# Scratch tiles of the router in half a PSUM bank, a second buffer for positions, and another order of the last steps but one

## The chip, the cores and the metric

The kernel runs on one core of a Trainium2 chip, as one program. The metric is the device time of an execution in microseconds. The median before is 797.3 us of 3 runs (796.97 to 798.79).

## The reference

Two stages follow each other. The first is attention in which a query sees only the keys of its own hash bucket; its output is the input `x` of a mixture of experts in which each token goes to one of eight experts.

```python
# attention: q, k, v are (4, 8, 768, 64), proj is (64, 6)
q_bucket = sum((q @ proj > 0) * 2**arange(6))          # k_bucket likewise
scores = where(q_bucket == k_bucket, q @ k.T / 8, -1e9)
attn = softmax(scores, eps=1e-9) @ v
x = attn.transpose(0, 2, 1, 3).reshape(3072, 512)
# experts: w_gate (512, 8), w1 (8, 512, 1024), w2 (8, 1024, 512)
logits = x @ w_gate + modality_bias[modality_id]
e_idx = argmax(logits); gate_w = softmax(logits, eps=1e-9)[e_idx]
out[e_idx == e] = gate_w * (relu(x @ w1[e]) @ w2[e])   # for each expert e
```

## The kernel before

**Attention.** There are 4 batches of 8 heads; two heads make a pair, so there are 16 pairs `i`, four to a batch. A loop over `i` and six key tiles `kt` runs a string of letters for each `kt` (`PLAN`, line 36; `PLAN0` for the first pair). Each letter issues one step. `S` (`score`, lines 281, 282) is a score matmul with its exponential on ScalarE (lines 293, 300); GpSimd adds the exponentials up into `sp` (line 303). `M` (`maxp`, lines 225, 231) is a matmul for the next pair, whose row maximum VectorE reduces out of a PSUM tile `psm`; there are two such tiles. `B` (`maxp_back`, lines 250 to 253) turns these maxima round on TensorE and lets VectorE write `a_0g`, `a_1g` and the flags `lone`. `T` and `P` prepare the operands of the pair after next. `A` (`weigh`, lines 322, 327) multiplies the exponentials of one key tile by `v`: first the 512 columns in the tile `psu0`, then the other 256 columns in `psu1`; ScalarE copies both to `ut` (line 332) at the end of a pair. `psu1` fills half of its PSUM bank. `Q` (`sums`, line 345) sums `sp`.

**Router.** When the four pairs of a batch are done, `finish(b)` and `route(b)` work out logits, the chosen expert and the position of every token in a table. They are generators, and a letter takes them one step on. The steps are: 1 and 2 the products with `w_gate` (line 361), 3 the sums turned round (line 371), 4 the reciprocal (373), 5 and 6 the logits of each head (386), 7 their sum `lg` (389), 8 the maximum `rm`, the difference `rd` and its exponential `rex` on ScalarE, 9 the one-hot choice `rw`, `rwm`, `oh`, 10 the matmuls 602 and 604 that count tokens, then `rk` and the counts `run`, 11 the softmax sum `rsum`, 12 the positions `pos` and, as integers, `posi`. Six more steps write six columns of records to the table `tab` in DRAM by an indirect DMA that GpSimd issues (`put`, line 624). For batches 0 and 1 these six go to a list `later`, of which the letter `s` takes one at a time; the last one of batch 1 comes in pair 13, `kt` 4. Nearly all of this is VectorE work on tiles of 6 to 48 elements a partition.

**The last batch but one.** `finish_last` (line 412) takes batch 2 through steps 1 to 12, then runs `early_slots` in six steps (13 `above`, 14 `cumulate`, 15 to 17 `assign`, 18 `early`): which experts get the two slots of 512 tokens that start before batch 3 is routed. Then `early_tables` (line 707) loads these slots' rows of `tab`, and the six `put` steps follow. Which letters take a step is in `FIN` (line 44): one row for pairs up to 11, one for pairs 12 to 15, one entry for each pair of a batch.

**What sets the order.** In attention the order on TensorE and on SyncE's DMA queue is that of the letters. On VectorE, ScalarE and GpSimd a planner sets it beforehand from its own costs and from the order in which the program names the work; a step of the router is put behind the newest reduction or flag (`newest`). Each engine then takes its instructions strictly in that order. A pool with one buffer makes the writer of a new tile wait for all readers of the old one; instructions of different engines on one PSUM tile are ordered by waits, by tile and bank and not by column. `experts` follows: slots `("e", 0)` and `("e", 1)`, into whose first the steps of batch 3 are woven, then those of the late slots.

Of the kernel before, what the change touches and what calls it, by code (L numbers as in the profile page):

```python
# [28 lines left out]
P = 128  # L29
# [6 lines left out]
PLAN = (  # L36
    "LvSPMSMSfMTfexyhk",
    "SMSMVfSMAAQTesyghk",
    "SMTSMSMlGEfxyk",
    "SMTSMSMAAFGEekk",  # L40
    "SMSMTSMgfExeshk",
    "SMTSMTSMBAABFGFfFfggehksk",
)
FIN = (("G", "g", "h", "k"), ("FG", "f", "eE", "eE"))
AHEAD = 2
PLAN0 = (
    "LvSPMSMSMT",
# [29 lines left out]
    }  # L77


def attention(ctx, actx, tc, a, x_d, route, setup, early_slots, early_tables, latest, adds, bias, later):  # L80
    nc = tc.nc
    v = a["v"]
    NPR = a.get("npair", NP)
# [231 lines left out]
    def weigh():  # L315

        for i in range(NPR):
            t = st[i]
            t["u"] = [ps_u.tile([P, MAIN], F32, name=f"psu{j}") for j in range(2)]
            for part in range(2):  # L320
                w = COLS[part].stop - COLS[part].start
                nc.tensor.matmul(t["u"][part][:, 0:w], vsb[i % 2], t["lone"][:, COLS[part]], start=True, stop=False, skip_group_check=True)
            for kt in range(NT):
                for part in range(2):
                    w = COLS[part].stop - COLS[part].start
                    for h in range(2):
# [25 lines left out]
    def finish(b):  # L352
# [26 lines left out]
        for w in range(2):  # L379
# [5 lines left out]
                nc.tensor.transpose(tp[:, j], gsb[:, tt * P:(tt + 1) * P], ident)  # L385
            nc.vector.tensor_tensor(out=gl[:, ts, 0:8], in0=tp[:, 0:n].rearrange("p t (h r) -> p t h r", r=16)[:, :, :, 0:8], in1=rin[:, ts].unsqueeze(3).broadcast_to([P, n, 8, 8]), op=ALU.mult)
            yield
        lg = bp.tile([P, NT, 8], F32, name="lg")
        nc.vector.tensor_reduce(out=lg, in_=gl.rearrange("p t h e -> p t e h"), axis=AX.X, op=ALU.add)
        yield  # L390
        yield from route(b, lg, ps_x)
# [43 lines left out]
    with tc.manual_schedule(engines={mybir.EngineType.PE, mybir.EngineType.SP}):  # L435
# [98 lines left out]
def router(ctx, tc, a, x_d, tab):  # L534
# [43 lines left out]
            nc.gpsimd.tensor_copy(out=run[0], in_=base)  # L578
            nc.gpsimd.tensor_copy(out=recs[:, :, :, 0], in_=tok)

    scattered, latest, adds, later = [], [], [], []

    def route(b, lg, ps):
        l = lg
        m = wk.tile([P, NT], F32, name="rm")
        nc.vector.tensor_reduce(out=m, in_=l, axis=AX.X, op=ALU.max)
        d = wk.tile([P, NT, E], F32, name="rd")
        nc.vector.tensor_tensor(out=d, in0=l, in1=m.unsqueeze(2).broadcast_to([P, NT, E]), op=ALU.subtract)
        ex = wk.tile([P, NT, E], F32, name="rex")
        nc.scalar.activation(ex, d, AF.Exp)  # L590
        yield
        w = wk.tile([P, NT, E], F32, name="rw")
        nc.vector.scalar_tensor_tensor(out=w, in0=d, scalar=0.0, in1=rev.unsqueeze(1).broadcast_to([P, NT, E]), op0=ALU.is_ge, op1=ALU.mult)
        wm = wk.tile([P, NT], F32, name="rwm")
        nc.vector.tensor_reduce(out=wm, in_=w, axis=AX.X, op=ALU.max)
        oh = wk.tile([P, NT, E], BF16, name="oh")
        nc.vector.tensor_tensor(out=oh, in0=w, in1=wm.unsqueeze(2).broadcast_to([P, NT, E]), op=ALU.is_equal)
        yield
        pp = ps.tile([P, HALF], F32, name="psx")
        for j in range(NT):  # L600
            lhs = tri if j == 0 else onesb
            nc.tensor.matmul(pp[:, j * E:NT * E], lhs, oh[:, 0:NT - j].rearrange("p t e -> p (t e)"), start=(j == 0), stop=False, skip_group_check=True)
        for j in range(NT):
            nc.tensor.matmul(pp[:, 64:64 + E], onesb, oh[:, j], start=False, stop=(j == NT - 1), skip_group_check=True)
        rk = wk.tile([P, NT, E], F32, name="rk")
        nc.vector.tensor_tensor(out=rk, in0=pp[:, 0:NT * E].rearrange("p (t e) -> p t e", e=E), in1=run[b % 2].unsqueeze(1).broadcast_to([P, NT, E]), op=ALU.add)
        nc.vector.tensor_tensor(out=run[(b + 1) % 2], in0=run[b % 2], in1=pp[:, 64:64 + E], op=ALU.add)
        yield
        rec = recs[:, b]
        sm = wk.tile([P, NT], F32, name="rsum")  # L610
        nc.vector.tensor_reduce(out=sm, in_=ex, axis=AX.X, op=ALU.add)
        nc.vector.tensor_scalar(out=sm, in0=sm, scalar1=1e-9, scalar2=None, op0=ALU.add)
        nc.vector.reciprocal(rec[:, :, 1].bitcast(F32), sm)
        yield
        nc.vector.tensor_tensor(out=rk, in0=rk, in1=oh, op=ALU.mult)
        pos = wk.tile([P, NT], F32, name="pos")
        nc.vector.tensor_reduce(out=pos, in_=rk, axis=AX.X, op=ALU.add)
        posi = wk.tile([P, NT], I32, name="posi")
        nc.vector.tensor_copy(out=posi, in_=pos)
        yield  # L620

        def put(t):
            with tc.issue_after(latest[0]) if b < B - 1 else nullcontext():
                ins = nc.gpsimd.indirect_dma_start(out=tab, out_offset=bass.IndirectOffsetOnAxis(ap=posi[:, t:t + 1], axis=0), in_=rec[:, t], in_offset=None).ins
            for other in scattered:
# [12 lines left out]
    early = const.tile([P, E], F32, name="early")  # L638

    def above(cnt, row, name):  # L640
        g = wk.tile([P, E, 12], F32, name="sg")
        nc.vector.tensor_tensor(out=g, in0=cnt.unsqueeze(2).broadcast_to([P, E, 12]), in1=step[:, row], op=ALU.is_gt)
        nb = wk.tile([P, E], F32, name=name)
        nc.vector.tensor_reduce(out=nb, in_=g, axis=AX.X, op=ALU.add)
        return nb

    def cumulate(nb, name):
        c2 = wk.tile([P, E, E], F32, name="sc2")
        nc.vector.tensor_tensor(out=c2, in0=low, in1=nb.unsqueeze(1).broadcast_to([P, E, E]), op=ALU.mult)
        cu = wk.tile([P, E], F32, name=name)  # L650
        nc.vector.tensor_reduce(out=cu, in_=c2, axis=AX.X, op=ALU.add)
        cx = wk.tile([P, E], F32, name=name + "x")
        nc.vector.tensor_tensor(out=cx, in0=cu, in1=nb, op=ALU.subtract)
        return cu, cx

    def assign(n, cu, cx, first, size, out):

        sel = wk.tile([P, n, E], F32, name=f"sel{n}")
        sl = slot[:, 0:n].unsqueeze(2).broadcast_to([P, n, E])
        nc.vector.tensor_tensor(out=sel, in0=cu.unsqueeze(1).broadcast_to([P, n, E]), in1=sl, op=ALU.is_gt)  # L660
        t = wk.tile([P, n, E], F32, name=f"selx{n}")
        nc.vector.tensor_tensor(out=t, in0=cx.unsqueeze(1).broadcast_to([P, n, E]), in1=sl, op=ALU.is_gt)
        nc.vector.tensor_tensor(out=sel, in0=sel, in1=t, op=ALU.subtract)
        nc.vector.tensor_tensor(out=t, in0=sel, in1=eid.unsqueeze(1).broadcast_to([P, n, E]), op=ALU.mult)
        r = wk.tile([P, n], F32, name=f"selr{n}")
        nc.vector.tensor_reduce(out=r, in_=t, axis=AX.X, op=ALU.add)
        nc.vector.tensor_copy(out=out[:, 0], in_=r)
        yield
        w = wk.tile([P, E], F32, name="selw")
        if size:  # L670
            nc.vector.tensor_tensor(out=w, in0=first, in1=cx, op=ALU.subtract)
        else:
# [11 lines left out]
    eslot = const.tile([P, 2, EARLY], I32, name="eslot")  # L684

    def early_slots():
        nb = above(run[EARLYB % 2], 0, "enb")
        yield
        cu, cx = cumulate(nb, "ecu")
        zero = wk.tile([P, E], F32, name="ezero")  # L690
        nc.vector.memset(zero, 0.0)
        yield
        yield from assign(EARLY, cu, cx, zero, TS, eslot)
        nc.vector.tensor_scalar(out=early, in0=cx, scalar1=-1.0, scalar2=float(EARLY), op0=ALU.mult, op1=ALU.add)
        nc.vector.tensor_scalar(out=early, in0=early, scalar1=0.0, scalar2=None, op0=ALU.max)
# [36 lines left out]
        nc.vector.tensor_copy(out=tot[:, 2:3], in_=over[:, 0:1])  # L732
        return big, sml, tot

    return route, early_slots, early_tables, (eslot, etb, ete), late_slots, setup, latest, adds, bias, later


def experts(ctx, tc, a, x_d, tab, out, ps_x, ident, first, adds):
# [247 lines left out]
def body(tc, a, out):  # L986
# [1 line left out]
    x_d = tc.dram_tile([N + 1, DM], F32, name="x_d")  # L988
    tab = tc.dram_tile([DUMMY + TS, 2], I32, name="tab")
    with ExitStack() as ctx, ExitStack() as actx:  # L990
        route, early_slots, early_tables, early_tiles, late_slots, setup, latest, adds, bias, later = router(ctx, tc, a, x_d, tab)
        finish, finish_x, ps_x, ident = attention(ctx, actx, tc, a, x_d, route, setup, early_slots, early_tables, latest, adds, bias, later)
        actx.close()
        runner, tabs, conditional = experts(ctx, tc, a, x_d, tab, out, ps_x, ident, early_tiles, adds)
        r = runner()
# [38 lines left out]
```

## Time and profile before

| | |
|---|---|
| median of 3 runs | 797.3 us |
| the profiled execution's own time | 798.82 us |
| its span, first to last instruction | 796.9 us |
| mean granted TensorE clock | 0.983 |
| TensorE matmuls busy | 751.4 us (94%) |
| VectorE busy | 486.7 us (61%) |
| ScalarE busy | 415.0 us (52%) |
| GpSimd busy | 444.6 us (56%) |

PE is TensorE's matmuls, PEld its weight loads, DVE VectorE, ACT ScalarE, POOL GpSimd, SP SyncE. A row of the timeline gives start, length, engine, line, operation, the tile written and read, the count, and in brackets how long the engine sat idle before it and what ended that. In a table by stretches, each engine has its busy time, and PEclk is the granted TensorE clock as a share of full speed. Attention takes the span up to about 481 us, the experts the rest.

### The profile page before, as it was taken

To read this page: it belongs to the slowest core of one execution; us is meant where nothing else is said; L and a number is where in the kernel's file an instruction comes from. 1 tells how busy PE (TensorE), PEld (TensorE's weight loads), DVE (VectorE), ACT (ScalarE), POOL (GpSimd) and SP (SyncE) were. 2 spreads that over 40 slices of the span, in tenths; PEclk is the share of its full clock that TensorE was granted. 3 is DMA by queue.
4 is the path that set the end of the run, shared out by engine and by line. 5 is a ranking of instruction groups with operands and counts; after the bars stand their busy time and mean duration, and the time that the engine had idled before them with its cause. 6 is when DMAs were issued, how large, how long until landed. Compare 5 with 4: busy or idle time off the path is not lost.

```text
span 796.9 us, 11622 instructions
## 1 busy us (share of the span) xinstructions
PE 751.4 (94%) x4060; PEld 523.7 (66%) x4060; DVE 486.7 (61%) x828; ACT 415.0 (52%) x732; POOL 444.6 (56%) x325
## 2 busy tenths in 40 slices
PE   5799999999999999999898899999999999999996
PEld 2555556556566566555555556878888888888885
DVE  5677677577777769766857758754244342752422
ACT  3666676666557566665554455324253334643323
POOL 7298988788879988789775793024220204202002
PEclk9699999999999999999999999999999999999999
DMA  5676544254347434454400366466443435853411
GB/s 193 157 181 160 159 122 133 65 159 113 111 120 177 115 81 125 117 168 108 120 21 14 83 143 233 150 82 223 132 160 90 161 103 170 267 143 121 132 55 60
DMA packets 59573, 104.11 MB, mean 131 GB/s; under 512 B 9709, under 2 KB 30957, under 8 KB 59504
## 3 DMA queue, kind: packets, MB, share of 16 engines
q1 hardware_dynamic: 53424, 88.10, 39.8%
q0 software_dynamic: 4928, 13.14, 5.2%
q10 hardware_dynamic: 1152, 2.03, 0.8%
q8 instruction: 34, 0.56, 0.3%
q14 instruction: 35, 0.29, 0.1%
HBM read 59.76 MB, written 13.33 MB: 92 GB/s over the span
## 4 chain that ended last, share of the span: by engine, by line
PE 64%; DVE 11%; issue 10%; ACT 6%; DMA 4%; POOL 2%; SPq 1%; another core or an unknown queue 1%; ACTq 0%; POOLq 0%; DVEq 0%
PE psu L327 12%; PE pss L281 8%; PE pss L282 6%; PE hps L824 5%; PE hps L825 5%; PE hps L826 5%; PE yps L868 4%; PE yps L870 4%; PE yps L869 4%; PE psm L225 3%; ACT pb L293 2%; PE psm L231 2%; DVE b_1g L162 2%; DVE a_0g L252 2%; DVE mx L227 1%
## 5 line engine op out<-in xcount | busy, mean ns | idle before, releaser
L303 POOL TENSOR_TENSOR sp<-sp,pb 128x768 f32<-128x768 f32 x124 | 232.4, 1900 | 33.0 <-ACT pb L300 30.5
L293 ACT ACTIVATE pb<-pss 128x512 f32<-128x512 f32 x192 | 114.2, 598 | 112.3 <-PE pss L282 96.2
L227 DVE TENSOR_REDUCE mx<-psm 128x1 f32<-128x512 f32 x192 | 130.6, 688 | 58.8 <-PE psm L225 57.7
L777 DVE TENSOR_TENSOR w<-raw,w 128x1024 fp32r<-128x1024 f32 x64 | 79.5, 1248 | 95.3 <-ACT w L775 63.0
L327 PE MATMUL psu<-pb,vt 128*64 128x512 f32 (+1 forms) x768 | 137.0, 499 | 0.0
L775 ACT CAST w<-raw 128x1024 fp32r<-128x1024 f32 x64 | 66.9, 1050 | 73.3 <-PE yps L870 62.7
L327 PEld LDWEIGHTS psu<-pb,vt 128*64 128x64 f32 x768 | 51.6, 139 | 71.1 <-issue 61.3
L795 POOL DMA_INDIRECT xg<-x_d,tb x18 | 21.9, 1219 | 117.8 <-DMA tb<-tab 113.6
L281 PE MATMUL pss<-a_0g 128*128 128x512 f32 x192 | 80.8, 421 | 2.6 <-ACT pb L293 1.6
L868 PE MATMUL yps<-w,hl 128*128 128x512 f32 x208 | 82.7, 398 | 0.0
L870 PE MATMUL yps<-w,hh 128*128 128x512 f32 x208 | 81.3, 391 | 0.0
L869 PE MATMUL yps<-w,hh 128*128 128x512 f32 x208 | 81.0, 389 | 0.0
L824 PE MATMUL hps<-xh,w 128*128 128x512 f32 x192 | 75.5, 393 | 0.0
L825 PE MATMUL hps<-xl,w 128*128 128x512 f32 x192 | 74.8, 390 | 0.7 <-DVE xl L814 0.7
L826 PE MATMUL hps<-xh,w 128*128 128x512 f32 x192 | 74.8, 390 | 0.0
L303 POOL TENSOR_TENSOR sp<-pb,pb 128x768 f32<-128x768 f32 x31 | 56.7, 1850 | 29.7 <-ACT pb L300 29.6
L233 DVE TENSOR_REDUCE mx<-psm 128x2 f32<-128x512 f32 x96 | 66.1, 689 | 10.2 <-PE psm L231 7.5
L281 PE MATMUL pss<-a_1g 128*128 128x512 f32 x192 | 68.3, 356 | 3.9 <-ACT pb L300 3.9
L830 ACT ACTIVATE hh<-hps 128x512 fp32r<-128x512 f32 x48 | 28.7, 598 | 74.0 <-PE hps L826 71.9
L282 PE MATMUL pss<-b_0g 128*128 128x512 f32 x192 | 66.0, 344 | 0.8 <-DMA b_0g<-a_0g 0.8
L282 PE MATMUL pss<-b_1g 128*128 128x512 f32 x192 | 65.7, 342 | 0.0
L831 DVE SCALAR_TENSOR_TENSOR hl<-hps,hh 128x512 fp32r<-128x512 f32 x48 | 33.0, 688 | 51.4 <-ACT hh L830 49.1
(203 smaller groups left out, 1363.0 us busy)
## 6 DMA issues: line engine op xcount, KB each, us to landing
raw<-moe_w SPq DMA_DIRECT2D x64, 512.0 KB
xt<-qk SPq DMA_DIRECT2D x31, 384.0 KB
vt<-v SPq DMA_DIRECT2D x16, 384.0 KB
a_0g<-hx SPq DMA_DIRECT2D x30, 192.0 KB
a_1g<-hx SPq DMA_DIRECT2D x30, 192.0 KB
x_d<-xs SPq DMA_DIRECT2D x18, 256.0 KB
b_1g<-a_1g SPq DMA_DIRECT2D x17, 192.0 KB
b_0g<-a_0g SPq DMA_DIRECT2D x17, 192.0 KB
```

Of the source, the lines that this page charges most:

```text
L227: newest[:] = [nc.vector.tensor_reduce(out=mx[:, qt + j, 1 - h, 0:1], in_=mp, axis=AX.X, op=ALU.max).ins]
L281: nc.tensor.matmul(out, t["s1"][h][:, ks], t["m1"][h][:, cs], start=True, stop=False)
L282: nc.tensor.matmul(out, t["s2"][h][:, ks], t["m2"][h][:, cs], start=False, stop=True)
L293: nc.scalar.activation(t["pb"][kt][:, h, 0:MAIN], sp, AF.Exp, scale=0.125)
L303: add = (nc.vector if h and i in CFG["spd"] else nc.gpsimd).tensor_tensor(out=t["sp"][:, h], in0=(t["pb"][0] if kt == 1 else t["sp"])[:, h ...
L327: nc.tensor.matmul(t["u"][part][64 * h:64 * h + 64, 0:w], t["v"][:, h, kt], t["pb"][kt][:, h, COLS[part]], start=False, stop=(kt == NT - 1 ...
L824: nc.tensor.matmul(hps, lo[:, c, fs], xh[:, c], start=(c == 0), stop=False)
L825: nc.tensor.matmul(hps, hi[:, c, fs], xl[:, c], start=False, stop=False)
L826: nc.tensor.matmul(hps, hi[:, c, fs], xh[:, c], start=False, stop=(c == 3))
L868: nc.tensor.matmul(yps[g], hl[fc][:, gs], hi[:, fb], start=(fc == 0), stop=False)
L869: nc.tensor.matmul(yps[g], hh[fc][:, gs], lo[:, fb], start=False, stop=False)
L870: nc.tensor.matmul(yps[g], hh[fc][:, gs], hi[:, fb], start=False, stop=(fc == 7))
```

## The change

Four things are done.

The tile `psu1` becomes one lasting tile `shared` of a whole bank; `weigh` uses its columns 0 to 255 and the router's tiles lie in columns 256 to 511 while attention runs (`Spots`; with no PSUM given it falls back to the pool). After attention the router's work uses pool tiles as before. The instructions that produced and read these tiles are the same, but for three: batch 1 writes its counts a second time into the scratch (`counts`), `cumulate` reduces a second time into a pool tile, and `early` takes two instructions in place of three. Operands are placed so that no instruction has two tensor inputs in PSUM, and nearly none has two in SBUF.

`posi` gets a second buffer.

`PLAN` gets a letter `w` behind the `G` in `kt` 2, 3 (two) and 4. `FIN` changes its row for pairs 12 to 15: in pair 12 `w` takes a step in place of `F` and `G` (4 steps in place of 7), in pair 13 `f` and `e` in place of `f` alone (12 in place of 7). So pair 12 makes steps 1 to 4 (before 1 to 7), pair 13 steps 5 to 16 (before 8 to 14), and pair 14 begins with 17 (before 15).

```diff
-    "SMTSMSMlGEfxyk",
-    "SMTSMSMAAFGEekk",
-    "SMSMTSMgfExeshk",
+    "SMTSMSMlGwEfxyk",
+    "SMTSMSMAAFwGwEekk",
+    "SMSMTSMgwfExeshk",
...
-FIN = (("G", "g", "h", "k"), ("FG", "f", "eE", "eE"))
+FIN = (("G", "g", "h", "k"), ("w", "fe", "eE", "eE"))
...
+class Spots:
+    psum = None
+    def __call__(self, pool, shape, name, at):
+        if self.psum is None:
+            return pool.tile(shape, F32, name=name)
+        n = int(np.prod(shape[1:]))
+        ap = self.psum[:, at:at + n]
+        return ap if len(shape) == 2 else ap.rearrange("p (a e) -> p a e", a=shape[1])
...
+    shared = ps_u.tile([P, MAIN], F32, name="psu1")
+    spot.psum = shared[:, REST:MAIN]
...
-            t["u"] = [ps_u.tile([P, MAIN], F32, name=f"psu{j}") for j in range(2)]
+            t["u"] = [ps_u.tile([P, MAIN], F32, name="psu0"), shared[:, 0:REST]]
...
-        lg = bp.tile([P, NT, 8], F32, name="lg")
+        lg = spot(bp, [P, NT, 8], "lg", 0)
...
         sums(NPR - 1)
+        spot.psum = None
...
-        d = wk.tile([P, NT, E], F32, name="rd")
+        d = spot(wk, [P, NT, E], "rd", 48)
...
-        w = wk.tile([P, NT, E], F32, name="rw")
+        w = spot(wk, [P, NT, E], "rw", 96)
...
-        rk = wk.tile([P, NT, E], F32, name="rk")
+        rk = spot(wk, [P, NT, E], "rk", 144)
...
+        if b == EARLYB - 1:
+            counts.append(spot(wk, [P, E], "counts", 200))
+            nc.vector.tensor_tensor(out=counts[0], in0=run[b % 2], in1=pp[:, 64:64 + E], op=ALU.add)
...
-        sm = wk.tile([P, NT], F32, name="rsum")
+        sm = spot(wk, [P, NT], "rsum", 192)
...
-        pos = wk.tile([P, NT], F32, name="pos")
+        pos = spot(wk, [P, NT], "pos", 192)
...
-        posi = wk.tile([P, NT], I32, name="posi")
+        posi = wk.tile([P, NT], I32, name="posi", bufs=2)
...
-        cx = wk.tile([P, E], F32, name=name + "x")
-        nc.vector.tensor_tensor(out=cx, in0=cu, in1=nb, op=ALU.subtract)
+        cx = spot(wk, [P, E], name + "x", 224)
+        cs = cu
+        if spot.psum is not None:
+            cs = wk.tile([P, E], F32, name=name + "s")
+            nc.vector.tensor_reduce(out=cs, in_=c2, axis=AX.X, op=ALU.add)
+        nc.vector.tensor_tensor(out=cx, in0=cs, in1=nb, op=ALU.subtract)
...
-        nc.vector.tensor_scalar(out=early, in0=cx, scalar1=-1.0, scalar2=float(EARLY), op0=ALU.mult, op1=ALU.add)
-        nc.vector.tensor_scalar(out=early, in0=early, scalar1=0.0, scalar2=None, op0=ALU.max)
-        nc.vector.tensor_tensor(out=early, in0=early, in1=nb, op=ALU.min)
+        left = wk.tile([P, E], F32, name="eleft")
+        nc.vector.tensor_scalar(out=left, in0=cx, scalar1=-1.0, scalar2=float(EARLY), op0=ALU.mult, op1=ALU.add)
+        nc.vector.scalar_tensor_tensor(out=early, in0=left, scalar=0.0, in1=nb, op0=ALU.max, op1=ALU.min)
```

The tiles `sg`, `enb`, `sc2`, `ecu`, `ecux`, `sel`, `selr` and `selw` of `early_slots` go to the scratch in the same way.

## Rows read from the trace of the kernel before

**Rows 1.** The page's first part: busy time of each engine.

```profile
PE 751.4 (94%) x4060; PEld 523.7 (66%) x4060; DVE 486.7 (61%) x828; ACT 415.0 (52%) x732; POOL 444.6 (56%) x325
```

**Rows 2.** Busy time in stretches from one `Q` to the next: pairs 4, 12, 13, 14.

```profile
142.93:171.75 28.82, 27.63 (x171) 16.43 (x169) 20.17 (x36) 17.80 (x35) 22.66 (x15) 1.00 0.41 114
...
368.31:402.74 34.43, 30.61 (x190) 18.09 (x188) 23.26 (x46) 16.71 (x35) 28.84 (x21) 0.95 0.30 77
402.74:433.78 31.04, 27.15 (x157) 17.38 (x155) 20.84 (x51) 16.58 (x33) 20.34 (x16) 0.95 0.08 23
433.78:462.52 28.74, 26.09 (x145) 15.86 (x143) 21.67 (x38) 12.89 (x25) 21.16 (x14) 0.94 0.40 110
```

**Rows 3.** Timeline of PE, 385 to 442 us: its longest waits.

```profile
388.95 0.63 PE L385 MATMUL psx<-ident,gsb 128*128 128x128 f32 x4 [0.54 <-DVE lone L253]
390.17 0.41 PE L385 MATMUL psx<-ident,gsb 128*128 128x128 f32 x2 [0.59 <-DVE lone L253]
...
397.22 0.18 PE L602 MATMUL psx<-oh,tri 128*128 128x48 bf16 x1 [2.10 <-DVE oh L597]
...
424.84 0.34 PE L208 MATMUL psx<-bits,pat 128*128 128x384 bf16 x1 [3.50 <-DVE lone L253]
...
441.92 0.53 PE L231 MATMUL psm<-a_1g 128*128 128x256 f32 x2 [2.38 <-DVE mx L227]
```

**Rows 4.** Stretches right behind three waits: stretch, length, engines, PEclk, DMA, GB/s.

```profile
397.20:402.80 5.60, 5.58 (x38) 2.81 (x41) 1.19 (x4) 0.97 (x2) 3.57 (x2) 0.70 0.01 1
...
424.85:428.60 3.75, 3.75 (x16) 3.39 (x16) 3.33 (x10) 2.15 (x4) 0.00 (x0) 0.55 0.00 0
...
441.90:447.00 5.10, 5.08 (x20) 2.11 (x20) 3.34 (x9) 0.63 (x1) 2.87 (x2) 0.67 0.01 1
```

**Rows 5.** Timeline of DVE, 394 to 397 us.

```profile
394.04 1.20 DVE L588 TENSOR_TENSOR rd<-lg,rm 128x48 f32<-128x48 f32 x1
...
396.96 0.21 DVE L597 TENSOR_TENSOR oh<-rw,rwm 128x48 bf16<-128x48 f32 x1
```

**Rows 6.** Timeline of DVE, 424 us.

```profile
424.02 0.17 DVE L619 CAST posi<-pos 128x6 int32<-128x6 f32 x1 [4.18 <-DMA tab<-recs,posi]
424.10 0.68 DVE L253 TENSOR_SCALAR lone<-psx 128x512 fp32r<-128x512 f32 x1
```

**Rows 7.** Timeline of POOL, 419 to 480 us.

```profile
419.49 0.98 POOL L624 DMA_INDIRECT tab<-recs,posi  x1
...
437.62 7.15 POOL L303 TENSOR_TENSOR sp<-sp,pb 128x768 f32<-128x768 f32 x4 [2.32 <-ACT pb L300]
449.04 0.98 POOL L624 DMA_INDIRECT tab<-recs,posi  x1 [4.27 <-DMA x_d<-xs]
...
473.09 6.89 POOL L303 TENSOR_TENSOR sp<-sp,pb 128x768 f32<-128x768 f32 x3
```

**Rows 8.** Timeline of DVE, 433 to 445 us: four long small instructions.

```profile
433.64 1.69 DVE L674 SCALAR_TENSOR_TENSOR selw<-selw,ke 128x8 f32<-128x8 f32 x1
...
437.80 1.71 DVE L677 SCALAR_TENSOR_TENSOR selx<-kslot,selw 128x16 f32<-128x16 f32 x1
...
440.03 1.23 DVE L678 TENSOR_TENSOR selx<-selx,sel 128x16 f32<-128x16 f32 x1
...
443.55 1.25 DVE L681 CAST eslot<-selr 128x2 int32<-128x2 f32 x1
```

**Rows 9.** Three lines' instructions over all batches: shortest, median and longest ns.

```profile
L588 DVE TENSOR_TENSOR rd<-lg,rm x4: 198/203/1199, 196.2 to 503.7; 128x48 f32<-128x48 f32 x4
...
L606 DVE TENSOR_TENSOR rk<-psx,run x4: 196/202/208, 213.0 to 514.5; 128x48 f32<-128x48 f32 x4
...
L607 DVE TENSOR_TENSOR run<-run,psx x4: 150/152/153, 213.1 to 514.6; 128x8 f32<-128x8 f32 x4
```

**Rows 10.** Timeline of PE and ACT in pair 6, behind step 8 of batch 0.

```profile
196.90 2.80 PE L327 MATMUL psu<-pb,vt 128*64 128x512 f32 x16
...
197.61 0.24 ACT L590 ACTIVATE rex<-rd 128x48 f32<-128x48 f32 x1
```

**Rows 11.** Timeline of PE at the end of attention.

```profile
480.73 0.85 PE L345 MATMUL psx<-sp,ones 128*32 128x384 f32 x8
```

More of the change, by code (lines that the diff above doesn't have):

```diff
@@ L77, in host_layout, with attention @@
     }
-def attention(ctx, actx, tc, a, x_d, route, setup, early_slots, early_tables, latest, adds, bias, later):
+class Spots:
[6 more added lines that the diff above has]
+        return ap if len(shape) == 2 else ap.rearrange("p (a e) -> p a e", a=shape[1])
+def attention(ctx, actx, tc, a, x_d, route, setup, early_slots, early_tables, latest, adds, bias, later, spot):
     nc = tc.nc
@@ L579, in setup @@
             nc.gpsimd.tensor_copy(out=recs[:, :, :, 0], in_=tok)
-    scattered, latest, adds, later = [], [], [], []
+    scattered, latest, adds, later, counts, spot = [], [], [], [], [], Spots()
     def route(b, lg, ps):
@@ L640, in above @@
     def above(cnt, row, name):
-        g = wk.tile([P, E, 12], F32, name="sg")
+        g = spot(wk, [P, E, 12], "sg", 0)
         nc.vector.tensor_tensor(out=g, in0=cnt.unsqueeze(2).broadcast_to([P, E, 12]), in1=step[:, row], op=ALU.is_gt)
-        nb = wk.tile([P, E], F32, name=name)
+        nb = spot(wk, [P, E], name, 208)
         nc.vector.tensor_reduce(out=nb, in_=g, axis=AX.X, op=ALU.add)
@@ L647, in cumulate @@
     def cumulate(nb, name):
-        c2 = wk.tile([P, E, E], F32, name="sc2")
+        c2 = spot(wk, [P, E, E], "sc2", 96)
         nc.vector.tensor_tensor(out=c2, in0=low, in1=nb.unsqueeze(1).broadcast_to([P, E, E]), op=ALU.mult)
-        cu = wk.tile([P, E], F32, name=name)
+        cu = spot(wk, [P, E], name, 216)
         nc.vector.tensor_reduce(out=cu, in_=c2, axis=AX.X, op=ALU.add)
-        cx = wk.tile([P, E], F32, name=name + "x")
-        nc.vector.tensor_tensor(out=cx, in0=cu, in1=nb, op=ALU.subtract)
+        cx = spot(wk, [P, E], name + "x", 224)
[4 more added lines that the diff above has]
+        nc.vector.tensor_tensor(out=cx, in0=cs, in1=nb, op=ALU.subtract)
         return cu, cx
     def assign(n, cu, cx, first, size, out):
-        sel = wk.tile([P, n, E], F32, name=f"sel{n}")
+        sel = spot(wk, [P, n, E], f"sel{n}", 160)
         sl = slot[:, 0:n].unsqueeze(2).broadcast_to([P, n, E])
@@ L664, in assign @@
         nc.vector.tensor_tensor(out=t, in0=sel, in1=eid.unsqueeze(1).broadcast_to([P, n, E]), op=ALU.mult)
-        r = wk.tile([P, n], F32, name=f"selr{n}")
+        r = spot(wk, [P, n], f"selr{n}", 192)
         nc.vector.tensor_reduce(out=r, in_=t, axis=AX.X, op=ALU.add)
@@ L668, in assign @@
         yield
-        w = wk.tile([P, E], F32, name="selw")
+        w = spot(wk, [P, E], "selw", 232)
         if size:
@@ L686, in early_slots @@
     def early_slots():
-        nb = above(run[EARLYB % 2], 0, "enb")
+        nb = above(counts[0], 0, "enb")
         yield
@@ L733, in late_slots @@
         return big, sml, tot
-    return route, early_slots, early_tables, (eslot, etb, ete), late_slots, setup, latest, adds, bias, later
+    return route, early_slots, early_tables, (eslot, etb, ete), late_slots, setup, latest, adds, bias, later, spot
 def experts(ctx, tc, a, x_d, tab, out, ps_x, ident, first, adds):
@@ L990, in body @@
     with ExitStack() as ctx, ExitStack() as actx:
-        route, early_slots, early_tables, early_tiles, late_slots, setup, latest, adds, bias, later = router(ctx, tc, a, x_d, tab)
-        finish, finish_x, ps_x, ident = attention(ctx, actx, tc, a, x_d, route, setup, early_slots, early_tables, latest, adds, bias, later)
+        route, early_slots, early_tables, early_tiles, late_slots, setup, latest, adds, bias, later, spot = router(ctx, tc, a, x_d, tab)
+        finish, finish_x, ps_x, ident = attention(ctx, actx, tc, a, x_d, route, setup, early_slots, early_tables, latest, adds, bias, later, spot)
         actx.close()
```

## The prediction

> **What bounds the kernel now.** I read the engines' busy time first: TensorE's matmuls fill 94% of the span [rows 1], so the time is TensorE's work plus the holes in it. A gain must close a hole or raise the clock; busy time saved on VectorE alone gives nothing. Next I cut attention into stretches from one `Q` to the next, one a pair [rows 2]. Pair 4, a usual one with router steps, takes 28.82 us at full clock. Pair 12 takes 34.43, and pairs 12, 13 and 14 alone have a mean clock of 0.94 to 0.95. In these three runs the work that the change rearranges: batch 2's router and the early slots. The timeline of TensorE shows why they are slow [rows 3]: three long waits, 2.10, 3.50 and 2.38 us, each ended by VectorE, and two of 0.54 and 0.59. Behind each long one the granted clock sits between its two levels of 1.2 and 2.4 GHz: a mean of 0.70 over 5.60 us, 0.55 over 3.75 and 0.67 over 5.10 [rows 4]. Length times one minus clock gives 1.68, 1.69 and 1.68 us lost behind a wait. So the holes cost:
> - A, in pair 13 before the counting matmul (line 602): 2.10 + 1.68 = 3.78
> - B, at the start of pair 14 (line 208): 3.50 + 1.69 = 5.19
> - C, in pair 14 (line 231): 2.38 + 1.68 = 4.06
> - D, at the end of pair 12 (line 385): 0.54 + 0.59 = 1.13
>
> 14.16 us in all. The question is which of them the change closes, and what it opens.
>
> **The second buffer of `posi` (B).** The integer positions of batch 2 wait 4.18 us, and what ends the wait is the DMA that still reads those of batch 1 [rows 6]. Its issue on GpSimd stands at 419.49, 0.98 us long [rows 7]: the last `put` of batch 1, which the letters place in the same `kt` 4 of pair 13 as step 12. VectorE goes in order, so `lone` stands behind `posi` and starts at 424.10 [rows 6]; TensorE waits for `lone` to free its PSUM tile and starts at 424.84 [rows 3]. With two buffers batch 2 writes where nobody reads, and batch 3 takes the first buffer long after. `lone` then starts 4.2 us earlier, more than the wait is long. Nothing else is late there: the instruction before `posi` had ended by 419.84 (424.02 less 4.18). All of B goes: 5.19.
>
> **The scratch in PSUM (C, part of A).** Four small instructions of `early_slots` take 1.69, 1.71, 1.23 and 1.25 us on 2 to 16 elements [rows 8]. Lines of that size that read PSUM take 0.15 us, whatever GpSimd does; `rk` with one input in PSUM takes 196 to 208 ns in all batches, while `rd` with both inputs in SBUF takes 198 to 1199 [rows 9]. And the long ones lie beside additions on GpSimd: four from 437.62 to 444.77 [rows 7], and `selx` ends at 439.51 and at 441.26, `eslot` at 444.80, near the ends of the first, second and fourth (7.15 / 4 = 1.79 each). So these instructions wait out a GpSimd addition that reads SBUF. In hole C the two on `selx` are over by 1.71 + 1.23 - 2 x 0.17 = 2.6 us, as much as TensorE's 2.38; the reduction that it waits for stands behind them. With an operand in PSUM I expect 0.2 us each, and all of C goes: 4.06. In hole A `rd` is over by 1.0 [rows 5].
>
> What no row shows is VectorE writing PSUM. Nearest are the reads of rows 9: 0 to 10 ns dearer than the undisturbed SBUF form. I bound it by nothing and, as a long form, by the whole 0.2 us of such an instruction again; some 60 instructions are moved, of which about 20 lie in the crowded start of pair 14, so 0 to 4 us there. I take 0, by the nearest row.
>
> The Trainium skill has a rule against this (Perfetto Trace Analysis, Optimizing Scalar/DVE Operations): about 60 ns of overhead per VectorE instruction on SBUF and 125 on PSUM. The median `rk` of 202 against 203 ns of `rd` [rows 9] shows no such step for a read. By the rule 20 instructions would cost an estimated 1.3 us more, 787.7 in place of my 786.4.
>
> **The other rhythm (rest of A, D).** Before, steps 8, 9 and 10 follow each other in `kt` 0 and 1 of pair 13. The counting matmul stands ready at 395.12 (397.22 less 2.10), `oh` starts at 396.96 [rows 3, 5]; 1.0 us off `rd` would leave a hole of about 1.1. After, step 9 is at the end of `kt` 1 and the matmul at the end of `kt` 2, a whole key tile apart (about 28.8 / 6 = 4.8 us), so the rest closes too: A gives 3.78. Steps 4 to 7 leave `kt` 5 of pair 12, where line 385 met the tiles that `lone` still held; their place in `kt` 3 to 5 and in `kt` 0 of pair 13 lies 3 us behind `lone`. But the pattern matmul of the next pair then meets the same tiles. Between 0 and 1.13 I take half: 0.6.
>
> Together 5.19 + 4.06 + 3.78 + 0.6 = 13.6 us.
>
> **What it adds.** (1) Two instructions more, one less, on VectorE: one in all, of 0.15 us by the shortest line of [rows 9], in the start of pair 14: 0.15. (2) New waits. Scratch and `psu1` are now one tile in one bank, so the second part of each `A` waits for every scratch instruction named before it, and those named after it wait for the `A` and the copy to `ut`. A waiting `A` holds all of TensorE. I count 13 places where a scratch step lies between two groups of `A`: 4 in each of batches 0 and 1, 5 in the last. The nearest is step 8: before, `rex` in pair 6 ends at 197.85 [rows 10]; the first `A` there starts at 196.90, half of 2.80 us, its `psu1` part being the last third, thus at 197.83. So it is level. Elsewhere the letters leave most of a `kt`. I take 0.1 each, 1.3 us, between 0 and, where all were like the waits of D, 13 x 0.57 = 7.4. VectorE's own waits for `A` come where it has nothing else (behind `Q`). (3) Steps 14 to 17 crowd into the end of pair 13 and `kt` 0 of pair 14, beside `lone` and the reductions. Before, VectorE kept up there while TensorE ran at 0.55 clock [rows 4]; at full clock TensorE is 1.69 us sooner, so the cost is 0 to 1.7. I take 1.0. (4) `early_tables` moves from `kt` 3 of pair 14 to `kt` 2, `put` with it. On SP its two DMAs and the `x_d` writes queued behind come sooner; on GpSimd the first `put` waited 4.27 us at 449.04 [rows 7], which the row gives to `x_d`, but the DMA that reads `tab` had to land first, issued just before. (5) GpSimd's last three additions end at 479.98 [rows 7], 0.75 before the last `Q` [rows 11]. If TensorE comes 12 us sooner, they must as well. Between, GpSimd idles 2.32 + 4.27 [rows 7] and pair 14 has 21.16 busy of 28.74 [rows 2], so it can; I take 0.3, at most 3.
>
> Sum: 13.6 - 0.15 - 1.3 - 1.0 - 0.3 = 10.9 us off. What follows is TensorE-bound and moves along, its weight loads too, as they are freed by attention's end. The profiled execution took 798.8 (span 796.9 and 1.9 around it): 787.9 after. It lies 1.5 above the median of 797.3, so the forecast median is 786.4.
>
> **The rivals.**
> *Partly given back.* The holes close, but the 13 meeting places cost like D's waits (7.4) in place of 1.3: 10.9 - 6.1 = 4.8, 792.5. For it: steps of 20 small instructions before one `A`. Against: rows 10.
> *The scratch doesn't help.* The long small instructions wait for GpSimd wherever their operands lie. Then A (by the rhythm) and B close, C moves with its steps and stays: 10.9 - 4.1 = 6.8, 790.5. Against it stands the narrow spread of `rk`.
> *Slower: the shared bank takes TensorE into VectorE's queue.* Place: the second part of `A`, 13 times. Price: a wait like the shortest long one, 2.10 us, without loss of clock 27.3, against 13.6 gained: 13.7 slower, 811. It decides from a mean wait of 13.6 / 13 = 1.05 us. For it: VectorE is over 70% busy in these pairs (20.17 of 28.82 [rows 2]) and in order. Against: two `psm` tiles keep VectorE within two reductions of TensorE, and only step 8 stands right before an `A`.
> The Trainium skill (PSUM — Partial Sum Buffer, PSUM bank collisions raise a hardware error) says that engines on one bank are to be kept apart by bank and not by address; by that the waits exist though the columns differ. No run here shows their length yet.
>
> **How the numbers follow.** Forecast 0.66, by itself 783 to 790; partly given back 0.14; no help from the scratch 0.06; no change 0.04; slower 0.10. The low end is all 14.16 us off the median, 783.1, and a little: 782.8. The high end takes in the second rival and most of the first: 794.5. What is left out is mostly the slower case. A measurement can tell about 0.2% (1.6 us): faster 0.86, same 0.04, slower 0.10.
>
> **What would show it.** Right: pairs 12, 13 and 14 at about 30, 27 and 25 us with clock 1.00; no DVE row waiting for `tab`; `selw`, `selx`, `eslot` at 0.2 us; the last `Q` near 470. Wrong: waits of line 327 or 322 for `rd`, `rex`, `rk` or `pos` over 1 us; `put` or the last additions of GpSimd after 472 us with TensorE waiting at line 345; small instructions still over 1 us.

## The result, and the profile after

The changed kernel takes 789.88 us in the median of 6 runs (787.76 to 790.72) against 798.04 before: ratio 0.9891, 95% interval 0.9871 to 0.9910, 8.2 us off where 10.9 were forecast. A second series on another chip gave 790.54 against 797.36, ratio 0.9917 (0.9891 to 0.9942). The profiled execution took 790.72, span 788.9.

First, where in the span the 8.0 us between the two profiles (796.9 to 788.9) lie. The sums matmul `Q` runs once a pair; these are its first starts before and after, and the last one after (the last before is in [rows 11]).

```profile
63.22 0.85 PE L345 MATMUL psx<-sp,ones 128*32 128x384 f32 x8
```

```profile
61.35 0.85 PE L359 MATMUL psx<-sp,ones 128*32 128x384 f32 x8
...
472.89 0.85 PE L359 MATMUL psx<-sp,ones 128*32 128x384 f32 x8
```

From first to last `Q` it is 417.5 us before and 411.5 after: 6.0 us. Another 1.9 lie ahead of the first `Q`, where both programs issue the same instructions in the same order on every engine; there the profile before was at clock 0.54 from 20 to 30 us, the one after at 1.00. In the 14 profiles of this study the first `Q` starts between 61.2 and 64.9 us, whatever was changed. So 1.9 us of the difference is one execution against another, and below I compare the stretch from the first to the last `Q`. The pairs after (stretch, length, engines, granted clock), to be held against [rows 2]:

```profile
365.89:395.80 29.91, 28.01 (x177) 16.86 (x176) 21.35 (x41) 16.68 (x35) 27.12 (x19) 1.00 0.36 90
395.80:427.65 31.85, 28.11 (x168) 16.81 (x166) 21.85 (x63) 16.48 (x33) 23.69 (x18) 0.95 0.07 17
427.65:452.90 25.25, 24.20 (x145) 15.26 (x143) 17.28 (x30) 13.38 (x26) 19.62 (x15) 1.00 0.57 118
```

Pairs 12 and 14 lost 4.5 and 3.5 us and run at full clock, as forecast. Pair 13 did not get faster (31.04 to 31.85). TensorE's timeline after shows why; it answers to [rows 3]:

```profile
388.03 0.60 PE L399 MATMUL psx<-ident,gsb 128*128 128x128 f32 x4
...
393.93 1.94 PE L341 MATMUL psu<-pb,vt 128*64 128x256 f32 x12 [1.52 <-ACT rex L605]
...
399.53 0.20 PE L617 MATMUL psx<-oh,tri 128*128 128x48 bf16 x1
...
413.02 1.94 PE L341 MATMUL psu<-pb,vt 128*64 128x256 f32 x12 [0.74 <-DVE psu L662]
...
424.23 3.50 PE L341 MATMUL psu<-pb,vt 128*64 128x256 f32 x12 [2.61 <-DVE eslot L703]
...
452.90 0.84 PE L359 MATMUL psx<-sp,ones 128*32 128x384 f32 x4 [0.67 <-POOL sp L317]
454.65 0.84 PE L359 MATMUL psx<-sp,ones 128*32 128x384 f32 x4 [0.92 <-POOL sp L317]
```

None of the old waits is left: the transposes (line 399) and the counting matmul (line 617) start without one, and no matmul of pairs 12 to 14 waits 0.3 us or more for `lone` or a reduction. In their place the accumulating matmuls `A` wait three times, always with their second part, which lies in the bank that the scratch shares: for step 8 (`rex` reads `rd`), 13 (line 662) and 17 (line 703). Behind the longest the clock falls:

```profile
424.30:428.00 3.70, 3.70 (x17) 1.33 (x20) 0.00 (x0) 0.81 (x2) 0.45 (x1) 0.58 0.23 71
```

That is 3.70 x 0.42 = 1.55 us more. So 1.52 + 0.74 + 2.61 + 1.55 = 6.42 us are new, and 0.67 + 0.92 = 1.59 for GpSimd's additions, 8.01 in all. 14.16 closed less 8.01 opened is 6.15, near the 6.0 measured. VectorE's timeline, against [rows 6, 8]:

```profile
410.74 0.15 DVE L637 CAST posi<-psu 128x6 int32<-128x6 f32 x1
...
422.77 0.17 DVE L696 SCALAR_TENSOR_TENSOR psu<-psu,ke 128x8 f32<-128x8 f32 x1
...
423.19 0.17 DVE L699 SCALAR_TENSOR_TENSOR selx<-kslot,psu 128x16 f32<-128x16 f32 x1
...
424.01 0.16 DVE L703 CAST eslot<-psu 128x2 int32<-128x2 f32 x1
```

No wait for the table's DMA, and 0.17 us where there were 1.7.

### The profile page after: what moved, and what is told of

The parts are those of the page before. It is cut to its first block, busy times and chain, and to the rows that moved or that the text cites. A ratio compares the mean times of both kernels' runs of the same rounds, so it can differ in the third digit from the quotient of the medians.

```text
span 788.9 us, 11622 instructions
## 1 busy us (share of the span) xinstructions
PE 747.6 (95%) x4060; PEld 520.3 (66%) x4060; DVE 477.8 (61%) x829; ACT 414.8 (53%) x732; POOL 445.6 (56%) x325
## 4 chain that ended last, share of the span: by engine, by line
PE 65%; DVE 11%; issue 10%; ACT 5%; DMA 4%; POOL 3%; SPq 1%; POOLq 0%; ACTq 0%; DVEq 0%
PE psu L341 12%; PE pss L295 8%; PE pss L296 6%; PE hps L846 4%; PE hps L848 4%; PE hps L847 4%; PE yps L892 4%; PE yps L890 4%; PE yps L891 4%; PE psm L239 4%; PE psm L245 2%; ACT pb L307 2%; DVE b_1g L176 2%; PE psx L359 1%; DVE a_0g L266 1%
```

## The experiments

The kernel before took 797.2 to 797.4 us in the medians of the three series. "Wait" is what TensorE waits for VectorE's work in pairs 12 to 14 (waits from 0.3 us), "first to last" the stretch from the first to the last `Q`, both of the one profile.

| kernel | `posi` | scratch | letters | median | ratio (95%) | wait | first to last |
|---|---|---|---|---|---|---|---|
| before | 1 | no | old | 797.3 | 1 | 9.11 | 417.5 |
| changed, again | 2 | all | new | 790.54 | 0.9917 (0.9891 to 0.9942) | 4.86 | 411.7 |
| posi_alone | 2 | no | old | 796.27 | 0.9981 (0.9959 to 1.0002) | 8.04 | 414.7 |
| scratch_old_rhythm | 2 | all | old | 787.60 | 0.9865 (0.9835 to 0.9895) | 5.07 | 410.4 |
| rhythm_no_scratch | 2 | no | new | 788.32 | 0.9883 (0.9851 to 0.9915) | 2.64 | 407.7 |
| early_steps | 2 | all | earlier | 795.94 | 0.9982 (0.9965 to 0.9998) | 3.45 | 415.9 |
| step17_behind | 2 | all | one moved | 789.90 | 0.9901 (0.9881 to 0.9922) | 3.84 | 409.1 |
| spread_steps | 2 | all | spread | 784.78 | 0.9843 (0.9822 to 0.9865) | 1.50 | 403.5 |
| one_scratch | 2 | one output | new | 787.97 | 0.9880 (0.9860 to 0.9900) | 2.67 | 407.6 |
| input_scratch | 2 | one input | new | 785.30 | 0.9844 (0.9822 to 0.9866) | 0.77 | 405.9 |
| single_posi | 1 | all | new | 797.78 | 0.9999 (0.9980 to 1.0017) | 10.42 | 418.9 |
| spread_no_scratch | 2 | no | spread | 790.67 | 0.9898 (0.9872 to 0.9924) | 4.40 | 407.6 |
| spread_more | 2 | all | spread, one moved | 785.32 | 0.9847 (0.9824 to 0.9869) | 1.49 | 403.5 |

**The second buffer alone** (posi_alone).

```diff
-        posi = wk.tile([P, NT], I32, name="posi")
+        posi = wk.tile([P, NT], I32, name="posi", bufs=2)
```

> The kernel before with nothing but the second buffer of the integer positions. Theory (each hole closes by its own edit): hole B, 3.50 us of waiting and 1.69 us behind it at a lower clock, goes; holes A, C and D stay. So 5.2 us off the kernel before, 792.8 us against a median of 798.0, and no row of VectorE waits for the table's DMA. Rival (B only covers C: with lone sooner, VectorE meets GpSimd's additions at the same small instructions, and TensorE waits there as long): under 2 us off, 796 us or more, with the wait at the reductions' matmul (lines 225 to 231) grown from 2.38 us to over 4.

1.1 us off, at the edge of what can be told: the rival, with two waits of 2.46 and 2.34 us in place of one of over 4. TensorE's longest waits in this kernel, the granted clock behind each, and VectorE and GpSimd ahead of the second:

```profile
395.66 0.18 PE L602 MATMUL psx<-oh,tri 128*128 128x48 bf16 x1 [2.09 <-DVE oh L597]
...
423.72 0.51 PE L231 MATMUL psm<-a_0g 128*128 128x256 f32 x2 [2.46 <-DVE mx L227]
437.99 0.50 PE L231 MATMUL psm<-a_1g 128*128 128x256 f32 x2 [2.34 <-DVE mx L227]
```

```profile
395.70:401.00 5.30, 5.30 (x34) 2.85 (x33) 1.13 (x4) 0.85 (x2) 3.04 (x2) 0.68 0.00 2
...
424.00:429.00 5.00, 5.00 (x32) 3.46 (x33) 4.94 (x13) 2.11 (x5) 2.37 (x3) 1.00 0.15 56
...
438.00:443.00 5.00, 5.00 (x26) 2.64 (x27) 3.82 (x10) 1.23 (x2) 2.85 (x2) 1.00 0.01 1
```

```profile
420.39 2.66 DVE L642 TENSOR_TENSOR sg<-run,kstep 128x96 f32<-128x96 f32 x1
```

```profile
419.30 3.62 POOL L303 TENSOR_TENSOR sp<-sp,pb 128x768 f32<-128x768 f32 x2
```

`posi` and `lone` no longer wait, but step 13's first instruction behind them does: 2.66 us, until GpSimd's two additions end at 422.92. The wait that the DMA had caused was in series with one that GpSimd causes; taking one away shows the other.

**Scratch without the new letters, letters without the scratch.** The first takes PLAN and FIN from before, the second is the kernel before with `bufs=2` and the new PLAN and FIN.

> The changed kernel with the letters (PLAN and FIN) of the kernel before: scratch and second buffer without the rhythm. Theory 1 (the waits of the accumulating matmuls for the scratch, 1.52, 0.74 and 2.61 us in the changed kernel, come from where the new letters put steps 8, 13 and 17): other steps stand before an A here, so these three waits are gone or elsewhere; B and C close, a hole of about 1.1 us with 1.7 of clock stays before the counting matmul, and D's 1.13 us: about 788 to 792 us. Theory 2 (they come from sharing the bank, wherever the steps stand): waits of line 341 for VectorE of 4 us or more in all appear again beside the holes left of A and D, 793 us or more.

> The kernel before with the second buffer and the new letters, all small operands in SBUF. Theory 1 (the new waits are the price of the shared bank, the scratch's gain is hole C): no wait of the accumulating matmuls (line 327 here) for VectorE; the small instructions of steps 13 to 17 take over 1 us each again where GpSimd adds, and TensorE waits some 2 to 3 us (and loses 1.7 us of clock) for VectorE behind them. A and B gone, C back: 789 to 792 us, level with the changed kernel, since what the scratch gave (4.1 us) is what its bank took (6.4 us with its loss of clock). Theory 2 (the new waits come from the crowding of steps by the new letters, whatever memory the scratch is in): TensorE waits for VectorE at the same three places, 793 us or more.

Both are level with the changed kernel or a little faster. With the old letters the counting matmul waits 1.87 us, the transposes 0.55 and 0.59 (A and D), and `A` 1.39 and 0.67 for steps 15 and 17. Ahead of the counting matmul, VectorE now waits for ScalarE's `rex`, which reads `rd` in the same bank:

```profile
394.93 0.22 DVE L608 SCALAR_TENSOR_TENSOR psu<-psu,ke 128x48 f32<-128x48 f32 x1 [0.58 <-ACT rex L605]
```

```profile
396.40 0.18 PE L617 MATMUL psx<-oh,tri 128*128 128x48 bf16 x1 [1.87 <-DVE oh L612]
```

Without scratch no `A` waits for VectorE at all, and neither does the counting matmul; step 14's product takes 2.26 us, TensorE waits 1.98 behind it and 0.66 later, at full clock:

```profile
414.89 2.26 DVE L649 TENSOR_TENSOR sc<-klow,enb 128x64 f32<-128x64 f32 x1
```

```profile
417.81 0.51 PE L231 MATMUL psm<-a_0g 128*128 128x256 f32 x2 [1.98 <-DVE mx L227]
...
427.69 0.51 PE L231 MATMUL psm<-a_0g 128*128 128x256 f32 x2 [0.66 <-DVE mx L227]
```

By their waits theory 1 holds in both, though both times are a little under its ranges: with the new letters the scratch took what it gave, or more. Buffer and letters alone make up the whole gain of the changed kernel.

**Steps earlier** (early_steps): a letter `z` in place of pair 13's `f` and `e`, and two more `w` for pair 12.

```diff
-    "LvSPMSMSfMTfexyhk",
-    "SMSMVfSMAAQTesyghk",
-    "SMTSMSMlGwEfxyk",
-    "SMTSMSMAAFwGwEekk",
-    "SMSMTSMgwfExeshk",
-    "SMTSMTSMBAABFGFfFfggehksk",
+    "LvSPMSMSfzMTfzexyhk",
+    "SMSMVfSMAAQTzesyghk",
+    "SMTSMSMlGwzEfxyk",
+    "SMTSMSMAAFwzGwzEekk",
+    "SMzSMzTSMgwzfExewshk",
+    "SMTSMwTSMBAABzFGzFfFfggehksk",
...
-FIN = (("G", "g", "h", "k"), ("w", "fe", "eE", "eE"))
+FIN = (("G", "g", "h", "k"), ("w", "z", "eE", "eE"))
```

> The changed kernel with the steps of batch 2 earlier and clear of the accumulating matmuls: six steps in pair 12 instead of four; step 8 a quarter of a pair before an A, step 9 behind it, steps 13 to 15 in key tile 4 of pair 13, 16 and 17 right behind the A of key tile 5. Theory 1 (the changed kernel loses 1.52 + 0.74 + 2.61 us of waiting and 1.56 us of clock because steps 8, 13 and 17 are issued late and stand in VectorE's queue when an A wants the bank): all three waits fall under 0.3 us, and the time falls by about 6 us from the changed kernel's 789.9 to 783 to 785 us. Theory 2 (VectorE is full there and the waits only move to another place): the sum of TensorE's waits for VectorE in pairs 12 to 14 stays at 4 us or more, and the time within 2 us of 789.9.

Both theories miss: some 6 us slower than the changed kernel. None of its three waits recurs, but step 15 now stands ahead of the `A` of key tile 5, and VectorE takes its instructions between the two halves of `lone`:

```profile
418.96 2.78 PE L341 MATMUL psu<-pb,vt 128*64 128x256 f32 x12 [3.45 <-DVE eslot L689]
...
458.67 1.49 PE L359 MATMUL psx<-sp,ones 128*32 128x384 f32 x4 [3.34 <-POOL sp L317]
```

The clock behind the first is 0.66 over 5 us. GpSimd then idles 7.74 us for exponentials that come late, and its additions are 3.34 us late at pair 14's sums. Not how early a step is named counts, but whether VectorE has it done when the next `A` comes.

**Steps behind the `A`.** step17_behind moves one step, spread_steps all of batch 2 (a letter `z` for pair 13, `q` for pair 14).

```diff
-    "LvSPMSMSfMTfexyhk",
-    "SMSMVfSMAAQTesyghk",
-    "SMTSMSMlGwEfxyk",
-    "SMTSMSMAAFwGwEekk",
-    "SMSMTSMgwfExeshk",
-    "SMTSMTSMBAABFGFfFfggehksk",
+    "LvSPMSMSfzMTfzezxyhk",
+    "SMSMVfSMAAQzTezqqsyghk",
+    "SMqTSMSMlGwzEfxyk",
+    "SMTSMSMAAFwzqGwzqEekk",
+    "SMzqSMTSMgwfExeqshk",
+    "SMTSMTSMBAABzqFGqFfqFggehksk",
...
-FIN = (("G", "g", "h", "k"), ("w", "fe", "eE", "eE"))
+FIN = (("G", "g", "h", "k"), ("w", "z", "q", "eE"))
```

> The changed kernel with one step moved: step 17 stands behind the two A of key tile 1 of pair 14 instead of at the end of key tile 0. Theory (the changed kernel's wait of 2.61 us at that A is the price of sharing the bank with a step that VectorE reaches late, and the 1.56 us behind it come with it): the wait goes and 2.6 to 4.2 us with it, 785.7 to 787.3 against 789.9; VectorE waits for the copy of the sums instead, where nobody waits for VectorE. Rival (VectorE is full there, TensorE waits for it wherever the step stands): the reductions' matmul (line 245) waits instead, and the time stays within 1.5 us of the changed kernel's.

> The changed kernel with every scratch step of batch 2 placed behind an A: step 8 and 9 behind those of key tile 1 of pair 13, 11 and 12 of key tile 3, 13 early in key tile 4, 14 behind those of key tile 5, 15 and 16 behind those of key tile 1 of pair 14, 17 early in key tile 2, 18 and the tables' loads behind those of key tile 3. Theory (price of the shared bank is paid where a step stands within VectorE's delay ahead of an A): waits of line 341 for VectorE sum to under 1 us, 783 to 786 us. Rival (as the steps that were moved earlier showed: the order that the planner gives VectorE puts small steps ahead of what an A needs in any rhythm): waits of 3 us or more, 788 us or more.

> The changed kernel once more, beside the three others on one chip. All theories: within 0.2% of 789.9 us in the median; its profile shows again waits of the accumulating matmuls for VectorE at the same places (1.5, 0.7 and 2.6 us), since these follow from the order of the instructions; the loss of clock behind the last of them may or may not appear, as the run with the second buffer alone showed full clock behind two waits of 2.3 to 2.5 us.

The changed kernel repeats its waits (1.51, 0.74, 2.61, clock 0.83 from 420 to 430 us) and its stretch (411.7). With step 17 alone behind the `A`, that wait falls only to 1.59, now for step 16, with the clock kept (neither theory: it stays at the `A` but does not go); the stretch is 2.5 us shorter, the median 0.6, which these runs can't tell from nothing. With all steps behind the `A` no row of line 341 waits for VectorE; one wait of the shared bank is left, and the time is 784.8, 12.6 us under the kernel before and better than both kernels:

```profile
429.06 0.39 PE L336 MATMUL psu<-lone,vs 128*128 128x256 f32 x1 [1.50 <-DVE eslot L703]
```

> The run with the spread steps with one step moved again: step 17 from early key tile 2 of pair 14 to behind the A of key tile 1, right behind step 16. There, the second part of the A's start in key tile 3 waited 1.50 us for step 17's last instruction. Theory (the price is VectorE's delay: it reaches step 17 1.5 us late): the wait falls under 0.4 us and the time by about 1.3 us, 783.5. Rival (VectorE works at the pace of the reductions there, small steps between them end when the reductions end): the wait stays over 1 us and the time within 0.5 us of 784.8.

The rival: 785.32, and 1.49 us of wait. VectorE's rows there alternate, one reduction of 0.67 and one small instruction, so step 17 ends when they end.

**Does the scratch give anything then?** The spread letters with everything in SBUF.

> The letters of the run with the spread steps, which took 784.8 us, with all small operands in SBUF again. Theory 1 (there the letters had put the price of the bank away and left the scratch's gain): small instructions take 1 to 2 us again beside GpSimd's additions, TensorE waits 2 to 4 us for VectorE behind them, 787 to 790 us. Theory 2 (the letters alone made that run fast, the scratch gives nothing where steps are spread): within 1.5 us of 784.8, with waits for VectorE of under 2 us in all.

Theory 1, a little above its range: 790.67, 5.9 us slower than with scratch; waits of 0.86, 1.49, 0.35, 0.92 and 0.78 us, with small instructions of up to 1.81 us ahead of them.

**Which operand has to be in PSUM?** Both kernels are rhythm_no_scratch with one tile moved: one_scratch the output of step 14's product, input_scratch its second input.

```diff
-        c2 = wk.tile([P, E, E], F32, name="sc2")
+        c2 = spot[0][:, 0:E * E].rearrange("p (a e) -> p a e", a=E) if spot else wk.tile([P, E, E], F32, name="sc2")
```

```diff
+        nbp = spot[0][:, 0:E]
+        nc.vector.tensor_reduce(out=nbp, in_=nb.unsqueeze(2), axis=AX.X, op=ALU.add)
+        cu, cx = cumulate(nb, "ecu", nbp)
...
-        nc.vector.tensor_tensor(out=c2, in0=low, in1=nb.unsqueeze(1).broadcast_to([P, E, E]), op=ALU.mult)
+        nc.vector.tensor_tensor(out=c2, in0=low, in1=nbp.unsqueeze(1).broadcast_to([P, E, E]), op=ALU.mult)
```

> The new letters and the second buffer, and of all scratch only one tile in PSUM: the 8 x 8 product of step 14 (sc2). Without scratch its instruction took 2.26 us beside a GpSimd addition, and TensorE waited 1.98 us behind it. Theory (what waits out GpSimd's addition is a small instruction with all operands in SBUF; one operand in PSUM frees it, and far from an A it costs nothing): this instruction takes 0.2 us, the wait of 1.98 us goes, the sum of the waits of TensorE for VectorE in pairs 13 and 14 falls from 2.64 us to about 0.7, and the time from 788.3 to about 786. Rival (the next small instruction with operands in SBUF takes the wait over, as in the run with the second buffer alone): one of the instructions behind it takes over 1 us, TensorE waits 1.5 us or more there, 787.5 us or more.

> As the run with one tile of scratch, but the other side of the instruction: the 8 x 8 product of step 14 is written to SBUF, and its second input, the 8 numbers before it, is read from a copy in PSUM that one more reduction writes. With the product written to PSUM and both inputs in SBUF that instruction took 2.29 us and TensorE waited 2.02 us. Theory 1 (what waits out GpSimd's addition is an instruction that reads all its tensors from SBUF; where it writes doesn't matter): now 0.2 us, and the wait of 2.0 us is gone or under 0.5; the stretch from the first sums to the last, 407.6 us in the profile of that run, falls to 405 to 406. Theory 2 (it waits as soon as one operand of two is in SBUF, and what helped in the changed kernel was that the small instructions stand elsewhere in time): it takes over 1 us again and the wait of about 2 us stays.

GpSimd and VectorE with the output in PSUM, then the same with the input there:

```profile
415.70 3.62 POOL L305 TENSOR_TENSOR sp<-sp,pb 128x768 f32<-128x768 f32 x2
...
417.12 2.29 DVE L652 TENSOR_TENSOR psu<-klow,enb 128x64 f32<-128x64 f32 x1
```

```profile
416.46 3.64 POOL L305 TENSOR_TENSOR sp<-sp,pb 128x768 f32<-128x768 f32 x2
...
418.60 0.20 DVE L653 TENSOR_TENSOR sc<-klow,psu 128x64 f32<-128x64 f32 x1
```

Both run beside two additions. An output in PSUM changes nothing (2.29 us, the wait of 2.02 stays: my expectation was wrong); an input there takes the wait away. So theory 1 of input_scratch holds. That one tile of 8 numbers, with the letters and the buffer, gives 785.3 us, level with the best.

**The single buffer in the changed kernel** (single_posi): `bufs=2` taken out.

> The changed kernel with a single buffer for the integer positions. Theory (hole B stood on two waits in series: the table's DMA, and behind it small instructions that wait for GpSimd; the second buffer alone gave 1.1 us because the latter then showed): with the scratch in place the DMA's wait shows alone, a row of VectorE waits for the table's DMA and TensorE for VectorE behind it, 2 to 4 us slower than the changed kernel, 792 to 794. Rival (with the new letters the last put of batch 1 is long done when positions of batch 2 are due): no such row, within 0.2% of 789.9.

7.2 us slower than the changed kernel on the same chip, and level with the kernel before: the direction of the theory at twice its price. `posi` waits 4.02 us for the table's DMA, step 13 stands behind it, and `A` waits for step 13's bank, 6.37 us, with clock 0.60 over the next 5.0. So the shared bank makes the same DMA dearer than in the kernel before, where TensorE waited 3.50 us; what a single buffer costs with the new letters and no scratch was not run.

```profile
418.64 0.17 DVE L637 CAST posi<-psu 128x6 int32<-128x6 f32 x1 [4.02 <-DMA tab<-recs,posi]
```

```profile
419.93 3.68 PE L341 MATMUL psu<-pb,vt 128*64 128x256 f32 x12 [6.37 <-DVE psu L662]
```

## Why the prediction was right, and where it was wrong

The time lies in the range, 3.5 us above the forecast of 786.4 and 2.6 below the 792.5 of the rival "partly given back": it is nearer to that rival. What the change closes came out as a sum; what it opens cost 8.0 us where 2.75 were counted (0.15, 1.3, 1.0 and 0.3). That the time is still in the range is owed to the range's high end, which took in most of that rival, and in so far to luck.

- **The holes** (13.6 of 14.16 us): all four closed, D wholly where I took half. Right as a sum.
- **Hole by hole** it was wrong: "Nothing else is late there ... All of B goes: 5.19". The second buffer alone gave 1.1, for behind `posi` stood an instruction that waits for GpSimd. B and C are one chain. The buffer alone does not close it, and scratch and letters without the buffer give nothing (ratio 0.9999). With the buffer, either the scratch or the new letters close most of it: of the 5.88 us that TensorE waited there, 2.06 are left with the scratch and the old letters, 2.64 with the letters and no scratch.
- **The scratch's part** of the gain (C, and 1.0 us of A) was not its own: buffer and letters alone take 788.3 us. Only with its steps behind the `A` did the scratch add something: spread_steps is 5.9 us faster than spread_no_scratch. Of A's 2.10 us the scratch without the letters left 1.87 where I had worked out about 1.1, for VectorE now waits 0.58 for `rex`; the letters alone closed A.
- **New waits of `A`** (2): the failing term. "only step 8 stands right before an `A`" and 0.1 at each of 13 places: 1.3. Three places cost 1.52, 0.74 and 2.61, with 1.55 of clock 6.4; the others cost nothing in sight, for the page's row of the line has 4.9 us of waiting over all 768 matmuls:

```profile
L341 PE MATMUL psu<-pb,vt 128*64 128x512 f32 (+1 forms) x768 | 136.8, 497 | 4.9 <-DVE eslot L703 2.6
```

Step 8 was called level and was 1.5 late; steps 13 and 17, with a good part of a key tile ahead of their `A`, were late because VectorE takes their small instructions one by one behind reductions and the work of `B`, as here for step 13:

```profile
411.97 0.69 DVE L266 SCALAR_TENSOR_TENSOR a_0g<-psx,a_0g 64x512 fp32r<-64x512 f32 x1
412.70 0.27 DVE L662 TENSOR_REDUCE psu<-psu 128x8 f32<-128x96 f32 x1
```

It is the mechanism of the rival "partly given back" (7.4), in fewer places at a higher price.

- **Crowding** (3), 1.0 us: it showed in these waits, not beside them; no reduction's matmul waits 0.3 us or more. The share "over 70% busy" that was read for VectorE is 67 to 75% in pairs 12 to 14 [rows 2].
- **Clock**: 1.68 us was counted behind each long wait. posi_alone has the same 1.70 behind 2.09 us, and none behind 2.46 and 2.34. So about 5 us of the gain were less sure than I took them for.
- **GpSimd's tail** (5): 0.3 forecast, 1.6 measured. The wait stands at pair 14's sums, one pair ahead of where I looked.
- **VectorE writing PSUM**: 0 was right. `rd` took 206 ns in the median against 203 [rows 9]. The rule cited from the Trainium skill (Perfetto Trace Analysis, Optimizing Scalar/DVE Operations), 60 against 125 ns of engine time and by that page about twice that in a profile, does not show in this row of the changed kernel (shortest, median, longest):

```profile
L603 DVE TENSOR_TENSOR psu<-psu,rm x3: 206/206/217, 194.4 to 393.4; 128x48 f32<-128x48 f32 x3
```

- The sum would have been 14.16 - 8.01 = 6.15 us; that the medians differ by 8.2 and 6.8 lies within what single executions differ at the start (some 3.7 us), but where the rest of the 8.2 lies was not shown.

## What to carry to other kernels

Before a hole is put down as a gain, look for the next wait that stands behind it in the same queue: two waits in series close only together, and whether a piece of a change adds anything is told by leaving that piece out. Scratch that shares a bank with an accumulation ties two engines' queues; place its steps right behind the accumulation's matmuls, and share as few steps as will do (here, with the new letters and the buffer, one input was enough). Against a wait of VectorE for GpSimd it is an input that has to leave SBUF, not the output.

## What the runs showed of the hardware

- A small VectorE instruction with both inputs in SBUF waits for GpSimd's additions, and now and then for the next one too: in one_scratch it started at 417.12, when the first of two additions had 0.4 us left (415.70 + 1.81), and ended at 419.41, after the second (419.32). The same in posi_alone, 423.05 against 422.92. The prediction had taken one addition, and most rows are like that: `selx` of [rows 8] ended at 439.51, with the first of four. What decides between the two is not shown.
- Its kinds: products, comparisons and differences of two SBUF tensors, and copies or scalar operations on one (a cast of 2 numbers took 1.53 us in rhythm_no_scratch, an operation on 8 with a constant 1.80 in input_scratch). A reduction did not: `rwm` (line 595 of rhythm_no_scratch) took 203 ns beside an addition at 196.9 us and 203 with none at 492.3. The Trainium skill (SBUF — State Buffer, Who interferes with whom) says as much: two SBUF inputs contend with a GpSimd instruction that reads SBUF, copies, casts and scalar operations can, and reductions never do. For two inputs its rule goes by where the inputs lie, and one_scratch and input_scratch agree.
- The clock's fall to the lower level does not follow the wait's length: waits of 2.09, 2.38, 2.61 and 3.45 us were followed by a mean clock of 0.68, 0.67 [rows 4], 0.58 and 0.66 over the 3.7 to 5.3 us behind them, others of 1.59, 2.02, 2.34 and 2.46 by 1.00. What decides it stays open.
